# A forget bias carried as three rows of the score product, one constant causal mask, and keys loaded once a head pair, in forgetting attention followed by a channel mix

## The chip, the cores and the metric

The kernel runs on one core of a Trainium2 chip. Time is device microseconds for one execution. The core's engines are TensorE (PE in the profile; its weight loads, which overlap its products, are PEld), VectorE (DVE), ScalarE (ACT), GpSimd (POOL) and SyncE (SP), which issues all transfers of this kernel on one queue. SBUF is the on-chip memory of 128 partitions, PSUM the memory that TensorE writes its products to.

## The reference, cut to what matters

```python
batch, n_heads, seq, head_dim = 8, 8, 576, 64      # d_model 512, d_ff 1024
def attn(q, k, v, s):
    scores = q @ k.T / sqrt(64)
    cum = cumsum(max(s, 0), axis=-1)
    bias = -(cum[:, :, :, None] - cum[:, :, None, :])      # query position minus key position
    scores = where(causal, -1e9, scores + minimum(bias, 0))
    scores = scores - max(scores); a = exp(scores); a = a / (sum(a) + 1e-9)
    return a @ v
def channel_mix(x):                    # x: heads side by side, 512 wide
    xk, xr = mixes of x and x one token earlier
    v = max(xk @ w_k, 0) ** 2 @ w_v
    return sigmoid(xr @ w_r) * v
```

All is float32. As s is clipped at zero, cum never falls, so inside the causal triangle the bias is cum[key] - cum[query], and the part that depends on the query alone drops out of the softmax: only cum[key] has to be added to a row of scores.

## The kernel before, in words

**Work.** There are 32 head pairs (8 batches, 4 pairs each). Batch 0 is visited in two parts, tiles A = (0, 1, 2) for all four pairs (visits 0 to 3) and then Z = (3, 4) (visits 4 to 7); batches 1 to 7 are visited once a pair. A head has five query tiles, of 64, 128, 128, 128 and 128 queries, starting at 0, 64, 192, 320 and 448; tile t sees the keys up to its own end, 64, 192, 320, 448 and 576 of them. The last is cut in two score tiles of 288 keys, so there are six score tiles a head. From batch 3 on (`PAIRED`) the heads are of a kind in which tiles 2 and 4 keep the weights of their last 64 keys at the front of the tile (`front`), so that two transposes can be taken as one. The channel mix runs in 18 chunks of 256 tokens, a chunk as soon as its tokens are there; its products are lines 1165 (hidden), 1207 (gate) and 1232 (output).

**Precision.** A matrix product takes two roundings. Each operand is split into a high part, rounded to fp32r (the format for fast products), and a low part, the rest. `split_qk` (line 637) makes for each head KH (k rounded, ACT, line 645), KL (the rest, POOL, line 649) and G, whose upper 64 partitions hold the rounded q (ACT, line 656) and whose lower 64 the rest of q (POOL, line 660). A head has 64 rows, so q and k are loaded twice, once on each half of the partitions (`load_turned`, line 624). A score tile is the sum of two products, G with KH and G with KL, each over all 128 rows (line 730). Visits 0 to 3 go another way: plain float32 products (line 719) with queries padded by zeros, and keys that are loaded once a pair.

**Bias and mask.** `prefix_sums` computes cum for all 64 heads at the start and stores it to DRAM (`cum_d`). Each later head gets its row back by a transfer that repeats it on all partitions (`cb`, 288 KB, line 682); heads 0 and 1 compute theirs directly (`first_sums`), heads 2 to 7 of batch 0 get theirs in two early loads (line 1319). POOL makes from cb the head's masks: cb with a large negative number above the diagonal (line 701). VectorE then reduces each score tile (line 757): it adds a row of cb left of the diagonal block and a row of the mask inside it, writes the sum to W and keeps the minimum of the negated scores in `nm`. These are two instructions where a score tile holds both kinds of columns, and each is followed by a short one that reads the accumulator. The exponent (ACT, line 775), the reciprocal of the sums (POOL and DVE, lines 815 and 820), the normalisation (POOL, line 791), the transposes (PE, lines 837 and 937), their splits (ACT and DVE, lines 866 to 924) and the products with v (PE, lines 986 and 1000) follow.

**Order.** Nothing waits in program order as written: every operation is handed to `Plan` with an estimated cost, what it reads and writes, and a due time. `Plan.run` simulates the engines twenty times, and emits all instructions in the order of the best simulation, so the order on each engine is fixed before the kernel runs, and a changed cost or operation can change it everywhere. While TensorE has nothing to do before its first steady work, the plan fills in dummy products (line 398). Buffers are named by a tag and a count of copies: KH, KL and G have three each, `raw` four, `cb` and `mask` two, and a writer waits for the readers of the copy that it takes.

Of the kernel before, what the change touches and what calls it, by code (L numbers as in the profile page):

```python
# [312 lines left out]
def forgetting_attention_then_channel_mix(  # L313
# [139 lines left out]
    cum_d = fixed(dram.tile([B * H, S], F32, name="cum_d"))  # L453

    def prefix_sums():
        cum = sbuf([B * H, S], "mask", 2)
        spos = sbuf([B * H, S], "mask", 2)
# [20 lines left out]
        dma(lambda: nc.sync.dma_start(cum_d.ap, cum.get()), [cum], [cum_d], 410)  # L478

    def first_sums(nk):  # L480
# [3 lines left out]
        cbs = [sbuf([P, nk], "cb", 2) for _ in range(2)]  # L484
# [9 lines left out]
        for j in range(2):  # L494
            dve(
                lambda j=j: nc.vector.tensor_tensor_scan(
                    out=cbs[j].get(), data0=ones.get(), data1=raw.get()[:, j], initial=0.0,
                    op0=ALU.mult, op1=ALU.add,
                ),
                [ones, raw], [cbs[j]], 2 * nk,  # L500
            )
        return cbs
# [111 lines left out]
    def load_keys(b, hp, e):  # L614
        x = sbuf([P, e], "KH", 3)
# [8 lines left out]
    def load_turned(src, b, hp, a, e):  # L624

        xs = [sbuf([P, e - a], "raw", 4) for _ in range(2)]
        for j in range(2):
            for r in range(2):
                dma(
                    lambda j=j, r=r: nc.sync.dma_start(  # L630
                        xs[j].get()[64 * r : 64 * r + 64], src[b, 2 * hp + j, :, a:e]
# [5 lines left out]
    def split_qk(qs, ks):  # L637

        nq, nk = qs[0].n, ks[0].n
        G = [sbuf([P, nq], "G", 3, F32R) for _ in range(2)]  # L640
        KH, KL = ([sbuf([P, nk], x, 3, F32R) for _ in range(2)] for x in ("KH", "KL"))
        for j in range(2):
            k, kh, kl = ks[j], KH[j], KL[j]
            act(
                lambda k=k, kh=kh: nc.scalar.copy(kh.get(), k.get()),  # L645
                [(k, 0), (k, 1)], [(kh, 0), (kh, 1)], nk, 90,
            )
            pool(
                lambda k=k, kh=kh, kl=kl: nc.gpsimd.tensor_tensor(  # L649
                    out=kl.get(), in0=k.get(), in1=f32(kh.get()), op=ALU.subtract  # L650
                ),
                [(k, 0), (k, 1), (kh, 0), (kh, 1)], [(kl, 0), (kl, 1)], nk, 210, 2.21,
            )
            q, g = qs[j], G[j]
            act(
                lambda q=q, g=g: nc.scalar.copy(g.get(), q.get()),
                [(q, 0), (q, 1)], [(g, 0), (g, 1)], nq, 90,
            )
            pool(
                lambda q=q, g=g: nc.gpsimd.tensor_tensor(  # L660
                    out=g.get()[64:P], in0=q.get()[64:P], in1=f32(g.get()[64:P]), op=ALU.subtract
# [5 lines left out]
    def scores(b, h, tiles, G, KH, KL):  # L667
# [137 lines left out]
        if 0 in tiles:  # L805
            mask(64, 0, 1)
# [652 lines left out]
```

## Time and profile before

| | us |
|---|---|
| median of 3 runs (859.77 to 861.87) | 860.07 |
| the profiled execution | 860.73 |
| its span | 858.9 |
| PE busy | 844.9 |
| PEld busy | 748.7 |
| DVE busy | 676.3 |
| ACT busy | 679.2 |
| POOL busy | 494.5 |

The profile is of one execution. A group of instructions is given as line, engine, operation, out<-in, shape and count, then the busy time in us, the mean of one in ns, and the idle time of the engine ahead of them with what ended it. Shapes are partitions by elements; for a product they stand behind rows by columns of the array. A product is pipelined, so what it costs in a stream is the time from its start to the next start, and its own duration is longer. A wait is given as engine, line, what was waited for, then the sum in us, the count and the longest.

### The profile page before, as it was taken

Reading aid. Unit: us, or ns where it says so; the run is one execution under the profiler, and the core shown is the slowest. Engines: PE = TensorE matmul, PEld = TensorE weight load, DVE = VectorE, ACT = ScalarE, POOL = GpSimd, SP = SyncE. Lnnn points to the kernel's source line nnn. Section 1 sums busy time; section 2 is a strip of 40 time slices with the busy share of each in tenths; the row PEclk is TensorE's granted clock in tenths of the full one; section 3 lists DMA queues with packets and bytes.
Section 4 is the critical chain, followed back from the end, with each engine's and each line's share of the span. In section 5 each row is a group of like instructions: output and inputs, shape, how many; then the busy total and the mean of one; then the engine's idle time right before and its main releaser. Section 6 shows DMA issues by size and latency. Waiting matters only on the chain.

```text
span 858.9 us, 18405 instructions
## 1 busy us (share of the span) xinstructions
PE 844.9 (98%) x5541; PEld 748.7 (87%) x5541; DVE 676.3 (79%) x2425; ACT 679.2 (79%) x1850; POOL 494.5 (58%) x854
## 2 busy tenths in 40 slices
PE   9979999999999999999999999999999999999998
PEld 8659789889898898989898989898989989988996
DVE  6988889989877998789878887888888789455431
ACT  3998999999988898789979797978897878445331
POOL 5897899997766757466665566456665652000000
PEclk9999999999999999999999999999999999999999
DMA  8879655564443545335343435252534220210100
GB/s 249 257 236 265 192 164 166 166 184 141 148 136 111 144 124 156 96 112 158 110 128 118 136 104 158 77 149 84 168 98 135 86 92 15 64 33 18 50 26 24
DMA packets 63108, 109.04 MB, mean 127 GB/s; under 512 B 10144, under 2 KB 24480, under 8 KB 63008
## 3 DMA queue, kind: packets, MB, share of 16 engines
q1 hardware_dynamic: 63008, 107.87, 42.7%
q8 instruction: 43, 0.70, 0.3%
q14 instruction: 57, 0.47, 0.2%
HBM read 88.80 MB, written 19.04 MB: 126 GB/s over the span
## 4 chain that ended last, share of the span: by engine, by line
PE 91%; ACT 3%; DMA 2%; DVE 1%; issue 1%; POOL 1%; SPq 0%; ACTq 0%; POOLq 0%; DVEq 0%
PE m L1232 21%; PE m L1165 19%; PE s L730 10%; PE m L1207 10%; PE po L1000 9%; PE t L837 9%; PE t L1232 2%; PE po L398 2%; PE po L986 2%; PE s L1165 2%; PE t L1165 2%; PE t L1000 1%; PE t L937 1%; PE s L719 1%; DMA w_v<-in_moe_w_v 1%
## 5 line engine op out<-in xcount | busy, mean ns | idle before, releaser
L1165 PE MATMUL m<-xh,w_k 128*128 128x256 f32 x976 | 200.3, 286 | 0.0
L775 ACT ACTIVATE W<-W,nm 128x448 f32<-128x448 f32 (+4 forms) x320 | 179.9, 563 | 25.2 <-DVE nm L757 22.4
L1232 PE MATMUL m<-w_v,kh 128*128 128x512 f32 x528 | 188.1, 406 | 0.0
L791 POOL TENSOR_SCALAR W<-W,rinv 64x64 f32<-64x64 f32 (+4 forms) x320 | 164.3, 532 | 12.6 <-DVE rinv L820 10.6
L1165 PEld LDWEIGHTS m<-xh,w_k 128*128 128x128 f32 x976 | 158.8, 189 | 1.4 <-DVE kl L1194 0.2
L837 PE MATMUL t<-ident,W 128*128 128x128 f32 (+1 forms) x736 | 134.7, 276 | 6.4 <-ACT ph L866 2.7
L1165 PE MATMUL m<-xl,w_k 128*128 128x256 f32 x488 | 139.7, 286 | 0.0
L649 POOL TENSOR_TENSOR KL<-raw,KH 128x576 fp32r<-128x576 f32 x64 | 91.6, 1432 | 80.1 <-ACT KH L645 75.4
L870 DVE TENSOR_TENSOR pl<-t,ph 128x512 fp32r<-128x512 f32 x224 | 107.1, 485 | 12.7 <-ACT ph L866 10.7
L837 PEld LDWEIGHTS t<-ident,W 128*128 128x128 f32 (+1 forms) x736 | 89.3, 137 | 27.0 <-ACT ph L903 5.2
L1232 PEld LDWEIGHTS m<-w_v,kh 128*128 128x128 f32 x528 | 98.1, 189 | 15.3
L730 PE MATMUL s<-KH,G 128*64 128x64 f32 (+2 forms) x360 | 110.7, 312 | 0.3 <-DVE nm L757 0.3
L757 DVE CUSTOM_DVE_ANT_0 W<-s,cb 128x64 f32<-128x64 f32 (+1 forms) x244 | 92.1, 381 | 17.9 <-PE s L730 15.4
L1232 PE MATMUL m<-w_v,kl 128*128 128x512 f32 x264 | 105.7, 400 | 0.0
L730 PE MATMUL s<-KL,G 128*64 128x64 f32 (+3 forms) x360 | 105.5, 297 | 0.0
L866 ACT CAST ph<-t 128x512 fp32r<-128x512 f32 x224 | 93.1, 424 | 12.5 <-PE t L837 10.5
L660 POOL TENSOR_TENSOR G<-raw,G 64x576 fp32r<-64x576 f32 (+1 forms) x64 | 85.8, 1341 | 27.6 <-issue 10.2
L1111 DVE SCALAR_TENSOR_TENSOR xp<-x,mu,xp 128x256 f32<-128x256 f32 (+3 forms) x184 | 76.3, 415 | 25.0 <-ACT xp L1104 22.5
L1104 ACT ACTIVATE xp<-x,mu 128x256 f32<-128x256 f32 (+3 forms) x184 | 77.6, 422 | 21.4 <-DMA x<-x_d 12.1
L1165 PEld LDWEIGHTS m<-xl,w_k 128*128 128x128 f32 x488 | 92.2, 189 | 0.8 <-DVE xl L1137 0.3
L1207 PE MATMUL m<-w_r,xh 128*128 128x512 f32 x264 | 92.6, 402 | 0.0
L757 DVE CUSTOM_DVE_ANT_0 W<-s,mask,nm 128x128 f32<-128x128 f32 x256 | 86.7, 344 | 3.1 <-POOL mask L701 0.5
(154 smaller groups left out, 1934.0 us busy)
## 6 DMA issues: line engine op xcount, KB each, us to landing
raw<-in_k SPq DMA_DIRECT2D x128, 144.0 KB, 3.2
cb<-cum_d SPq DMA_DIRECT2D x64, 288.0 KB, 3.6
raw<-in_q SPq DMA_DIRECT2D x112, 144.0 KB, 3.7
out<-g SPq DMA_DIRECT2D x36, 256.0 KB, 2.6
vn<-in_v SPq DMA_DIRECT2D x28, 320.0 KB, 3.3
x_d<-xT SPq DMA_DIRECT2D x28, 288.5 KB, 2.5
x<-x_d SPq DMA_DIRECT2D x11, 514.0 KB, 4.6
w_k<-in_moe_w_k SPq DMA_DIRECT2D x8, 512.0 KB, 5.5
```

Source lines behind the costliest of these rows:

```text
L649: lambda k=k, kh=kh, kl=kl: nc.gpsimd.tensor_tensor(out=kl.get(), in0=k.get(), in1=f32(kh.get()), op=ALU.subtract),
L730: lambda x=x, K=K: nc.tensor.matmul(ps.get()[:m, :w], G.get()[:, q0 : q0 + m], K.get()[:, k0 : k0 + w], start=x == 0, stop=x == 1,),
L757: lambda a=a, e=e, row=row, i=i, to=to: nc.vector.tensor_tensor_reduce(out=to(), in0=ps.get()[:m, a - k0 : e - k0], in1=row()[:m, a:e], sc ...
L775: lambda: nc.scalar.activation(W.ap[:m, :n], W.ap[:m, :n], AF.Exp, bias=nm.get()[:m, 3 * t + mi : 3 * t + mi + 1], scale=-1.0, accum_out=s ...
L791: lambda: nc.gpsimd.tensor_scalar(out=to.ap[:m, c : c + n], in0=W.ap[:m, :n], scalar1=rinv.get()[:m, t : t + 1], scalar2=1.0, op0=ALU.mult ...
L837: lambda: nc.tensor.transpose(ps.get()[0:m, place : place + P], pt[t].ap[:, k0 + front(t, tiles) : k0 + front(t, tiles) + m], ident.ap,),
L866: act(lambda: nc.scalar.copy(strips(ph), src()), [ps], [(ph, k) for k in ks], n * m)
L870: lambda: nc.vector.tensor_tensor(out=strips(pl), in0=src(), in1=f32(strips(ph)), op=ALU.subtract),
L1000: lambda: nc.tensor.matmul(po.get()[: P if both else 64, at + q0 - base : at + q0 - base + m], V.get()[:, kb, 2 * j : 2 * j + (2 if both e ...
L1165: lambda u=u, f=f, c=c, n=n, w=w, x=x: nc.tensor.matmul(ps.get()[:, u * CT : (u + 1) * CT], weight["k", c, f // 4].get()[:, w, f % 4 * P : ...
L1207: lambda c=c, n=n, x=x, w=w: nc.tensor.matmul(ps.get(), x.get()[:, c, ts], weight["r", c, 0].get()[:, w], start=c == 0 and n == 0, stop=c ...
L1232: lambda f=f, n=n, x=x, w=w: nc.tensor.matmul(ps.get(), x.get()[:, f, ts], weight["v", f, 0].get()[:, w], start=f == 0 and n == 0, stop=f ...
```

## The change

- `prefix_sums` also splits each prefix sum into three fp32r parts (two copies on ACT, two subtractions on VectorE) and stores them to DRAM as `cum3_d`, three rows a head.
- For visits 4 and later, `split_qk` makes other operands. QQ holds the rounded q on both halves of the partitions; K holds the rounded k on one half and the rest of k on the other. QL has the rest of q on 64 partitions and ones on three more (set once a buffer); KB has k, rounded by VectorE, on 64 partitions and the head's three rows of prefix sums on three more, loaded by a 6.75 KB transfer. A score tile is QQ with K over 128 rows plus QL with KB over 67 rows, and then holds scores and bias.
- With the bias in the product, the mask is the same for all heads: `lower`, built once, zero below the diagonal and the large negative number above it in its last 128 columns. The reduction of a score tile adds a slice of it, in one instruction, or in two where the last 64 columns are written to the front of the tile. The bias rows and masks of a head go, except in visits 0 to 3, which keep them in other buffers.
- Keys are loaded once a pair, 64 partitions for each of the two heads, in one transfer of 288 KB (160 KB in visits 0 to 3, as before) in place of four of 144 KB.

```diff
@@ prefix_sums
+        parts = [sbuf([B * H, S], x, 1, F32R) for x in ("w_v_2_0", "w_v_3_0", "xh1")]
+        for i, x in enumerate(parts):
+            if i < 2:
+                act(lambda x=x: nc.scalar.copy(x.get(), cum.get()), [cum], [x], S, 90)
+                dve(
+                    lambda i=i, x=x: nc.vector.tensor_tensor(
+                        out=(parts[2] if i else cum).get(), in0=cum.get(), in1=f32(x.get()),
+                        op=ALU.subtract,
+                    ),
+                    [cum, x], [parts[2] if i else cum], S,
+                )
+            dma(
+                lambda i=i, x=x: nc.sync.dma_start(cum3_d.ap[:, 2 - i], f32(x.get())),
+                [x], [(cum3_d, i)], 410,
+            )
@@ split_qk(b, hp, qs, k)
+            own, other = slice(64 * j, 64 * j + 64), slice(64 - 64 * j, P - 64 * j)
+            QQ, K = (sbuf([P, n], x, 3, F32R) for n, x in ((nq, "G"), (nk, "KH")))
+            QL, KB = (sbuf([P, S], x, 3, F32R) for x in ("QL", "KL"))
+            if made[0] < 3:
+                made[0] += 1
+                ahead(lambda QL=QL: nc.vector.memset(f32(QL.get()[64:67]), 1.0), (QL, 1), S)
+            dma(
+                lambda j=j, KB=KB: nc.sync.dma_start(
+                    f32(KB.get()[64:67, 0:nk]), cum3_d.ap[b * H + 2 * hp + j, :, 0:nk]
+                ),
+                [(cum3_d, i) for i in range(3)], [(KB, 1)], 40,
+            )
             act(
-                lambda k=k, kh=kh: nc.scalar.copy(kh.get(), k.get()),
+                lambda own=own, K=K: nc.scalar.copy(K.get()[own], k.get()[own]),
...
             pool(
-                lambda k=k, kh=kh, kl=kl: nc.gpsimd.tensor_tensor(
-                    out=kl.get(), in0=k.get(), in1=f32(kh.get()), op=ALU.subtract
+                lambda own=own, other=other, K=K: nc.gpsimd.tensor_tensor(
+                    out=K.get()[other], in0=k.get()[own], in1=f32(K.get()[own]), op=ALU.subtract
...
+            dve(
+                lambda own=own, KB=KB: nc.vector.tensor_copy(KB.get()[0:64, 0:nk], k.get()[own]),
+                [(k, j)], [(KB, 0)], nk, 1.92, 150, (2 * j, 0),
+            )
...
             pool(
-                lambda q=q, g=g: nc.gpsimd.tensor_tensor(
-                    out=g.get()[64:P], in0=q.get()[64:P], in1=f32(g.get()[64:P]), op=ALU.subtract
+                lambda x=x, QQ=QQ, QL=QL: nc.gpsimd.tensor_tensor(
+                    out=QL.get()[0:64, 0:nq], in0=x.get()[0:64], in1=f32(QQ.get()[0:64]),
+                    op=ALU.subtract,
...
+            found.append(((QQ, K, P), (QL, KB, 67)))
@@ scores: products
-            for x, K in enumerate((KH, KL) if KL is not None else ()):
+            for x, (G, K, n) in enumerate(() if CB else passes):
...
-                        G.get()[:, q0 : q0 + m],
-                        K.get()[:, k0 : k0 + w],
+                        G.get()[:n, q0 : q0 + m],
+                        K.get()[:n, k0 : k0 + w],
...
+            off = S - P - QS[t] if QS[t] < k0 + w else -k0
+            last = k0 + w - (f if QS[t] < k0 + w else 0)
+            for a, e, to in ((k0, last, k0 + f), (last, k0 + w, 0)):
+                if a < e:
+                    reduce(
+                        a, e, to, lambda a=a, e=e: lower.ap[:m, off + a : off + e], [lower]
+                    )
@@ load
-            loaded[n] = load_turned(q, b, hp, q0, q1), load_turned(k, b, hp, 0, q1)
+            loaded[n] = load_twice(b, hp, q0, q1), load_keys(b, hp, q1, "raw", 4)
@@ after prepare(0)
+    ahead(lambda: nc.vector.memset(lower.ap, 0.0), lower, S)
+    pool(
+        lambda: nc.gpsimd.affine_select(
+            out=lower.ap[:, S - P : S], in_=lower.ap[:, S - P : S], pattern=[[-1, P]], base=0,
+            channel_multiplier=1, compare_op=ALU.is_ge, fill=MASK * ISCALE,
+        ),
+        [], [lower], P, 137,
+    )
```

`ahead` is a small helper that hands an operation to VectorE with the earliest due time; `load_twice` is `load_turned` for q alone; `reduce` is the reduction of line 757 as a function.

More of the change, by code (lines that the diff above doesn't have):

```diff
@@ L453, in forgetting_attention_then_channel_mix @@
     cum_d = fixed(dram.tile([B * H, S], F32, name="cum_d"))
+    cum3_d = fixed(dram.tile([B * H, 3, S], F32, name="cum3_d"))
+    lower = fixed(const.tile([P, S], F32, name="lower"))
     def prefix_sums():
-        cum = sbuf([B * H, S], "mask", 2)
-        spos = sbuf([B * H, S], "mask", 2)
+        cum = sbuf([B * H, S], "x")
+        spos = sbuf([B * H, S], "xl0")
         ones = sbuf([B * H, S], "raw", 4)
@@ L483, in first_sums @@
         ones = sbuf([P, nk], "raw", 4)
-        cbs = [sbuf([P, nk], "cb", 2) for _ in range(2)]
+        cbs = sbuf([P, 2, nk], "xh0")
         dma(
@@ L496, in first_sums @@
                 lambda j=j: nc.vector.tensor_tensor_scan(
[L497 removed]
+                    out=cbs.get()[:, j], data0=ones.get(), data1=raw.get()[:, j], initial=0.0,
                     op0=ALU.mult, op1=ALU.add,
                 ),
[L500 removed]
+                [ones, raw], [(cbs, j)], 2 * nk,
             )
[L502 removed]
+        return [(cbs, 0), (cbs, 1)]
     def load_mu():
@@ L635, in load_turned, with ahead @@
         return xs
[L637 to L641, printed above, removed]
-        for j in range(2):
-            k, kh, kl = ks[j], KH[j], KL[j]
-            act(
-                lambda k=k, kh=kh: nc.scalar.copy(kh.get(), k.get()),
-                [(k, 0), (k, 1)], [(kh, 0), (kh, 1)], nk, 90,
+    made = [0]
+    def ahead(emit, what, n):
+        due, plan.due = plan.due, -2.0e5
+        dve(emit, [], [what], n)
+        plan.due = due
@@ L766, in products @@
                     ),
-                    [ps, (bias, t > 0 if own else part)] + ([(nm, (t, i - 1))] if i else []),
+                    [ps] + reads + ([(nm, (t, i - 1))] if i else []),
                     [(W, i), (nm, (t, i))], e - a, extra=143 if i else 78,
@@ L770, in products @@
                 i += 1
+            if CB:
+                if k0 < QS[t]:
+                    reduce(k0, QS[t], k0, lambda: bias_row()[:m, k0 : QS[t]], [(CB, part)])
+                own = slice(QS[t], QS[t] + m)
+                reduce(own.start, own.stop, own.start, lambda: M.get()[:m, own], [(M, t > 0)])
+                return i
+            off = S - P - QS[t] if QS[t] < k0 + w else -k0
[5 more added lines that the diff above has]
+                    )
             return i
@@ L803, in rs @@
             return x.get()[:, tiles[0] : tiles[-1] + 1]
-        if 0 in tiles:
+        if CB:
             mask(64, 0, 1)
-        mask(P, QS[max(1, tiles[0])], len([t for t in tiles if t]))
+            mask(P, QS[1], len(tiles) - 1)
         for t in tiles:
```

78 lines of the change are left out of this document (32 added, 46 removed).

## The prediction

> **What bounds the kernel now.** I read the page first (engines, slices, chain), then busy time by stage, then the waits of TensorE, then single groups.
>
> ```profile
> span 858.9 us, 18405 instructions
> PE 844.9 (98%) x5541; PEld 748.7 (87%) x5541; DVE 676.3 (79%) x2425; ACT 679.2 (79%) x1850; POOL 494.5 (58%) x854
> ...
> DMA  8879655564443545335343435252534220210100
> ...
> PE 91%; ACT 3%; DMA 2%; DVE 1%; issue 1%; POOL 1%; SPq 0%; ACTq 0%; POOLq 0%; DVEq 0%
> ```
>
> TensorE (PE) is busy 98% of the span and holds 91% of the chain that ended last. A modelled busy time alone would not prove that it runs at its peak, so I compare two places in the chain of waits in order of time: one in the middle, where attention and the channel mix are interleaved, and one near the end, where only the channel mix is left.
>
> ```profile
> 524.17 2.82 PE m L1165 x24
> ...
> 772.37 2.82 PE m L1165 x24
> ```
>
> 24 products of the same kind take 2.82 us in both places, 0.118 us each: in the middle TensorE is already at the rate of its undisturbed tail. The stages follow (length, then busy time of PE, PEld, DVE, ACT, POOL, granted clock, DMA share, GB/s):
>
> ```profile
> 18.00:42.00 24.00, 23.04 (x147) 16.45 (x145) 22.09 (x96) 21.57 (x79) 21.02 (x54) 1.00 0.87 272
> 42.00:62.00 20.00, 13.81 (x68) 10.39 (x69) 18.55 (x55) 19.23 (x55) 18.29 (x24) 0.91 0.74 222
> 62.00:120.00 58.00, 57.44 (x352) 48.04 (x352) 47.51 (x164) 53.52 (x138) 50.06 (x75) 1.00 0.79 220
> 120.00:330.00 210.00, 209.59 (x1429) 188.43 (x1428) 187.20 (x739) 194.17 (x546) 161.74 (x273) 1.00 0.51 146
> 330.00:740.00 410.00, 409.71 (x2711) 368.91 (x2710) 340.46 (x1262) 340.94 (x941) 235.23 (x401) 1.00 0.38 113
> 740.00:858.90 118.90, 115.15 (x685) 101.45 (x683) 49.96 (x86) 43.03 (x83) 0.00 (x0) 1.00 0.10 33
> ```
>
> So there are two kinds of stage. Until about 62 us TensorE waits for others: in 42 to 62 us it is busy 13.8 of 20 us while ACT is busy 19.2, DVE 18.6 and POOL 18.3. From 120 to 740 us its visible gaps are 0.7 us of 620. After 740 us there is no attention left, POOL is empty, and nothing that the change touches runs. The sum of TensorE's work does not depend on how fast the heads are served: a head that is ready sooner only lets a channel-mix product run later. The end moves only by what TensorE gains or loses in waiting, and by a change of its own work.
>
> **The change part by part.** The sum goes against the profiled execution, 860.73 us (span 858.9 and 1.8 us around it); it lies 0.66 us above the median of 860.07.
>
> *TensorE's products.* Each score tile keeps two products of the same widths: first (high part of q) with (high and low part of k), over 128 rows; then (low part of q, and three rows of ones) with (k, and three rows of prefix sums), over 67 rows instead of 128. The width sets the time, so I take 0. The nearest rows for a product with fewer rows are the plain value products of 64 rows, against the same with 128:
>
> ```profile
> 43.30 0.33 PE L986 MATMUL po<-ph,V 128*128 128x64 f32 x2
> 43.44 0.38 PE L730 MATMUL s<-KH,G 128*128 128x288 f32 x1
> ...
> 81.01 0.43 PE L986 MATMUL po<-ph,V 64*128 64x64 f32 x2
> 81.38 0.33 PE L837 MATMUL t<-ident,W 128*128 128x128 f32 x1
> ...
> L730 PE MATMUL s<-KL,G 128*64 128x64 f32 (+3 forms) x360 | 105.5, 297 | 0.0
> ```
>
> From start to next start the 128-row pair takes 0.14 us and the 64-row pair 0.37: 0.23 us more for going into the smaller row count and out again. The bounds are thus 0 and 0.23 us for each of the 360 second products, 83 us, with no cover, since TensorE is full. I take 0: 64 rows are half of the array's 128, 67 are more than half. The Trainium skill (TensorEngine Tiling (Array Packing), Tiling Modes) says that a change of tiling mode drains TensorE, and lists modes of 128, 64 and 32 rows, with the smaller ones for contractions up to 64. The trace agrees for 64 rows; by that list 67 rows are no change of mode and the term is 0, and a mode taken from the bare row count would give the 83 us.
>
> *VectorE's reductions.* Bias and mask no longer differ along a row, so the piece below the diagonal block and the block itself become one instruction where the output is contiguous.
>
> ```profile
> L757 DVE CUSTOM_DVE_ANT_0 W<-s,mask,nm 128x128 f32<-128x128 f32 x256 | 86.7, 344 | 3.1 <-POOL mask L701 0.5
> L757 DVE DVE_READ_ACCUMULATOR2_ANT nm<- 128x1 f32 x576 | 47.1, 82 | 0.0
> L757 DVE CUSTOM_DVE_ANT_0 W<-s,cb 128x320 f32<-128x320 f32 x64 | 31.1, 486 | 4.5 <-PE s L730 4.1
> L757 DVE CUSTOM_DVE_ANT_0 W<-s,cb 128x192 f32<-128x192 f32 x58 | 20.4, 352 | 5.5 <-PE s L730 4.8
> ```
>
> 320 against 192 columns cost 134 ns more, 1.05 ns a column. Merging saves the separate block (344 + 82 ns) and adds 128 columns (134 ns): 0.29 us a merge. Merges: four a head in batches 1 and 2 (16 heads), two in the paired batches 3 to 7 (40 heads; there tiles 2 and 4 still write their last 64 columns elsewhere) and two in the eight heads of visits 4 to 7. That is 64 + 80 + 16 = 160 merges, 46.7 us less.
>
> *VectorE's new copy of k* into KB, 64 a run. The nearest row has the same shape, one source, both sides in SBUF:
>
> ```profile
> L465 DVE TENSOR_SCALAR mask<-mask 64x576 f32<-64x576 f32 x1 | 0.5, 504 | 5.9 <-DMA mask<-in_s 5.9
> ```
>
> 64 by 0.50 us is 32.3 us more (up to 48 if it goes at the 1.05 ns a column of a reduction plus its 150 ns). VectorE's net is 14 us less at 0.50, nothing at the upper bound; per head 0.67 us less in batches 1 and 2, 0.08 less in the others.
>
> *POOL.* The masks go; the subtraction for k keeps its 576 columns on half the partitions, and its rows show that the partitions do not matter:
>
> ```profile
> L649 POOL TENSOR_TENSOR KL<-raw,KH 128x576 fp32r<-128x576 f32 x64 | 91.6, 1432 | 80.1 <-ACT KH L645 75.4 <-DMA x<-x_d 3.0 <-DVE rinv L820 0.4
> L660 POOL TENSOR_TENSOR G<-raw,G 64x576 fp32r<-64x576 f32 x56 | 79.9, 1427 | 26.6 <-issue 10.2 <-ACT G L656 9.5 <-DMA vn<-in_v 2.5
> L701 POOL TENSOR_SCALAR_AFFINE_SELECT mask<-cb 128x512 f32<-128x512 f32 x56 | 35.4, 632 | 0.3
> L701 POOL TENSOR_SCALAR_AFFINE_SELECT mask<-cb 64x64 f32<-64x64 f32 x58 | 13.5, 233 | 14.7 <-DMA cb<-cum_d 9.2 <-DVE cb L496 3.7 <-DVE nm L757 0.3
> ```
>
> 56 by (632 + 233) ns is 48 us less; the eight masks of 256 columns for visits 4 to 7 lie between the two rows, 3 us together. ACT's copies keep their widths: 0.
>
> *Transfers.*
>
> ```profile
> raw<-in_k SPq DMA_DIRECT2D x128, 144.0 KB, 3.2
> cb<-cum_d SPq DMA_DIRECT2D x64, 288.0 KB, 3.6
> ```
>
> Keys: 128 issues of 144 KB become 32 of 288 KB, 9.4 MB less. Bias: 64 of 288 KB become 64 of 6.75 KB, 18 MB less. About a quarter of the page's 109 MB goes, and 96 of SP's issues. The new small transfer waits on SP for a KL buffer where the bias transfer waited for a cb buffer.
>
> *What of this reaches the end, after 62 us.* These are the waits of TensorE (first three) and of its weight loads (the rest) in 65 to 740 us that name what is relieved:
>
> ```profile
> PE t L937 <- POOL W L791: 0.4, 1, 0.4
> PE s L730 <- DVE nm L757: 0.3, 1, 0.3
> PEld t L837 <- DVE pl L870: 2.1, 9, 0.4
> PEld t L937 <- POOL W L791: 0.8, 2, 0.6
> PEld s L730 <- DVE nm L757: 0.8, 3, 0.5
> ```
>
> Together 4.4 us: that is the most that can go. The chunk work fills most of what a late head leaves, and the paired heads, 40 of 64, get only 0.08 us of VectorE each, so I take 1.5 us off (bounds 0 and 4.4). What is late next in these tiles is the exponent on ACT, which is untouched.
>
> *Before 62 us.* Added at the start are two copies on ACT, four memsets, two subtractions on VectorE, an affine select on POOL and three stores on SP:
>
> ```profile
> L645 ACT CAST KH<-raw 128x576 fp32r<-128x576 f32 x64 | 43.0, 672 | 1.4 <-DMA raw<-in_k 0.9 <-PE s L730 0.6
> ACT w_k L577 <- DVE xh L571: 3.9, 1, 3.9
> L1194 DVE TENSOR_TENSOR kl<-m,kh 128x512 fp32r<-128x512 f32 x61 | 41.8, 685 | 4.9 <-ACT kh L1192 4.3
> L463 POOL MEMSET raw<- 64x576 f32 x1 | 0.6, 575 | 0.0
> 8.37 0.48 SPq L478 DMA_DIRECT2D cum_d<-mask  x1
> 12.36 1.71 SPq L1319 DMA_DIRECT2D w_v<-cum_d  x2
> 61.46 0.28 PE L1165 MATMUL m<-xh,w_k 128*128 128x256 f32 x1
> ```
>
> The copies are casts of 576 columns, 1.3 us, inside ACT's idle 3.9 us. The memsets, at 0.58 us each as on POOL, are 2.3 us of the 5.9 us in which VectorE waits for its first transfer (the L465 row above); the select costs less than the 632 ns of the wide mask, in the 3.7 us in which POOL waits for the first cb (the 64x64 mask row). Not covered are the subtractions, which fall where VectorE has no gap: 685 ns for 512 columns give 0.75 us, 1.5 us for the two. The stores, of the size of the one at 8.37 us, take 0.48 us of issue each, 1.4 us, and may stand ahead of the early bias loads at 12.36 us, behind which further q, k and weight loads queue. Bounds of the delay: 0 and 2.9 us; I take 1.0, since weight conversion can move into the holes. It counts in full only if it reaches the first channel-mix product at 61.46 us: from there on TensorE is never short of work. Visits 4 to 7 lose 3 us of POOL and 3 MB of transfers, but ACT, busy 19.2 of 20 us, keeps all of its work: I take 0.5 us off, between 1 us more (a different order) and 6.2 us less (all of TensorE's loss in that stage).
>
> Sum: 860.7 + 1.0 - 0.5 - 1.5 = 859.7, less 0.66 to the median: 859 us.
>
> **The rivals.**
>
> *No cover was needed (faster).* ACT, DVE, POOL and the queue are all nearly full before 62 us and feed each other, so a quarter less traffic and 3 us less POOL may loosen ACT too. For it: the DMA share is 0.87 in 18 to 42 us. Against it: ACT's own busy time. The Trainium skill (SBUF — State Buffer, Who interferes with whom) says that a copy of VectorE in its two-port mode shuts POOL out of SBUF while it runs; by that the eight copies for visits 4 to 7, 4 us, would take back POOL's 3 us there, and no row of this trace shows it. With half of the 6.2 us, and 3 of the 4.4, and no delay at the start: 860.1 - 3.1 - 3 = 854 us.
>
> *The start gets slower.* The prefix parts stand in front of the first heads on VectorE and SP, and the chain until 62 us takes the delay on. It decides when, with no gain later, more than 2.6 us of the 2.9 and of the 1 us for reordered visits come through: with all of it 860.1 + 2.9 + 1 = 864 us.
>
> *67 rows drain the array.* Each second product is then 0.23 us longer with its neighbours, and from 0.01 us on it decides the sign: 860 + 83 = 943 us. For it are the 64-row rows; against it that 67 rows are more than half of the array.
>
> *It doesn't do what it says:* VectorE's copy eats the merges (48 against 46.7 us) and the end does not move: that is in the forecast's own range.
>
> **How the numbers follow.** About 0.3% (2.6 us) is what a measurement tells from no change. Forecast, 857.5 to 862.6 us: 0.41. Faster rival: 0.39. Slow start: 0.13. Drain: 0.07. The likeliest is no change with a lean to the fast side, 858.7 (own range 856 to 862); the range runs from a little beyond the faster rival, 851, to beyond the slow start, 866; the drain is left out.
>
> **What would show it.** Right: no cb and mask instructions after visit 3; DVE busy some 10 to 15 us lower, POOL about 50 lower, PE's count and busy share the same; about 82 MB moved; 24 L1165 products still in 2.82 us. The start is read from the first L1165 product, at about 61.5 us now: each us there is a us at the end. Wrong: a longer start-to-start around the 67-row products, a first L1165 product beyond 63 or before 58 us, or PE waiting for KB's small transfer, which the forecast leaves at nothing.

## The result, and the profile after

The changed kernel takes 873.67 us (median of four runs, 873.47 to 874.64) against 860.97 for the kernel before beside it (859.77 to 863.14): ratio 1.0147, 95% interval 1.0123 to 1.0171. It is 12.7 us slower, where 858.7 was forecast. The profile page's first lines and the chain that ended last, by engine and by line (a view names a buffer, so KB stands there as KL, QQ as G and K as KH):

```profile
span 872.0 us, 17614 instructions
PE 855.7 (98%) x5536; PEld 753.6 (86%) x5536; DVE 700.8 (80%) x2175; ACT 689.3 (79%) x1852; POOL 455.9 (52%) x735
...
PE 72%; DVE 5%; ACT 2%; issue 1%; POOL 0%; DVEq 0%; ACTq 0%; POOLq 0%
PE m L1270 18%; PE m L1203 16%; PE m L1245 9%; PE s L766 8%; PE po L1038 7%; PE t L875 6%; PE t L1270 2%; PE s L1203 2%; PE t L1203 2%; DVE KL L692 1%; DVE W L781 1%; PE t L1038 1%; DVE pl L908 1%; PE t L975 1%; PE po L1245 1%
```

Less work is done (POOL 38.6 us less; 81.55 MB moved, not 109), but VectorE rose from 676.3 to 700.8 us, and VectorE now has 5% of the chain, with the new copy of k (KL L692) by name. The stages, with the columns of before:

```profile
42.00:62.00 20.00, 16.97 (x71) 13.09 (x71) 19.41 (x49) 18.39 (x52) 17.61 (x23) 0.74 0.61 199
62.00:120.00 58.00, 57.26 (x357) 48.99 (x355) 51.63 (x129) 54.29 (x137) 46.58 (x62) 1.00 0.46 136
120.00:330.00 210.00, 206.81 (x1389) 183.03 (x1388) 190.01 (x610) 192.40 (x535) 142.43 (x223) 1.00 0.33 100
330.00:740.00 410.00, 407.64 (x2678) 364.49 (x2677) 344.53 (x1156) 342.03 (x934) 215.85 (x342) 1.00 0.26 80
```

The first channel-mix product of TensorE in order of time, and two places of the chain of waits:

```profile
59.17 0.78 PE L1203 MATMUL m<-xh,w_k 128*128 128x256 f32 x1
```

```profile
581.74 2.86 PE m L1203 x24
...
755.48 2.85 PE m L1203 x24
```

Nothing is lost at the start: the first channel-mix product (L1203, L1165 before) comes at 59.17 us, 2.3 us earlier. At 0.74 the granted clock of 42 to 62 us is below the 0.91 of before, and still the start is not later; from 62 to 740 us it is 1.00 in both. The rate holds too: 24 of these products take 2.86 us in the middle and 2.85 in the tail. The 2.82 of before is no faster rate, as the kernel before has such groups of 2.85 and 2.87 too (at 576.58 and 625.56 us). From 120 to 740 us TensorE does 73 products fewer than the kernel before (4067 against 4140): it has lost time. Its visible gaps grew from 0.7 to 5.6 us, and the rest sits in waits that no gap shows, because a product's record (0.28 us for 256 columns) is longer than its 0.12 us of the stream. I add those up as *lost time*: from 120 to 745 us, each product's start to the next one's start, less what a product of its kind takes in an undisturbed stream (0.118 us for 256 columns, 0.134 for 288). Before 19.9 us, after 34.1: 14.2 more, about the 12.7 of the result. Only differences of this sum are used. The waits of TensorE and then of its weight loads, 65 to 740 us (sum in us, count, longest):

```profile
PE po L1038 <- DVE pl L908: 1.6, 4, 0.9
PE t L875 <- DVE xT L1076: 1.4, 2, 1.0
PE t L1038 <- DVE pl L908: 1.2, 1, 1.2
```

```profile
PEld po L1038 <- DVE pl L908: 4.6, 10, 1.3
PEld t L875 <- DVE pl L908: 2.9, 13, 0.3
PEld po L1038 <- ACT ph L904: 2.9, 13, 0.4
PEld t L875 <- DVE xT L1076: 2.7, 4, 1.4
```

These waits are for VectorE and ScalarE, in the steps after the softmax, few of which the change touches: ph and pl are the high and the low part of the transposed weights, xT is a head's output on its way to the channel mix. So something stands ahead of these steps in the queues of those engines. The 64 new copies by their line (shortest, median and longest in ns), and around the longest gap the chain of waits and the order of time on VectorE, GpSimd and TensorE:

```profile
L692 DVE CAST KL<-raw x64: 415/472/2917, 34.9 to 701.3; 64x576 fp32r<-64x576 f32 x64
```

```profile
208.53 1.99 DVE KL L692
```

```profile
208.45 2.07 DVE L692 CAST KL<-raw 64x576 fp32r<-64x576 f32 x1
210.64 0.28 DVE L908 TENSOR_TENSOR pl<-t,ph 128x128 fp32r<-128x128 f32 x1
...
206.88 1.67 POOL L829 TENSOR_SCALAR W<-W,rinv 128x448 f32<-128x448 f32 x3
208.50 1.71 POOL L621 TENSOR_TENSOR V<-vn,V 128x320 fp32r<-128x320 f32 x2
210.16 1.62 POOL L701 TENSOR_TENSOR QL<-raw,G 64x576 fp32r<-64x576 f32 x1
...
210.97 0.33 PE L1038 MATMUL t<-ph,V 128*128 128x128 f32 x1 [1.25 <-DVE pl L908]
```

Half of the copies take under half a microsecond, this one 2.07. It comes while a GpSimd instruction (L829) runs until 208.54, then waits out two subtractions that follow without a gap and end at 210.21, and ends 0.31 us after them; pl behind it starts at 210.64, and TensorE has stood 1.25 us for it. The 2917 ns copy lies beside two GpSimd instructions in the same way, and ends 0.3 us after the second. So it goes with nearly all: 24 copies take over 0.7 us, and 23 of them end 0.31 to 0.33 us after the end of a GpSimd instruction. Of the 12 places where the sum above loses over 0.25 us at once (7.2 us; before 2 places, 1.0 us), nine come within 4 us after a copy that took over 0.8 us.

### The profile page after: what moved, and what is told of

Read it like the earlier page. It is cut to its first block, busy times and chain, and to the rows that moved or that the text cites. A ratio compares the mean times of both kernels' runs of the same rounds, so it can differ in the third digit from the quotient of the medians.

```text
span 872.0 us, 17614 instructions
## 1 busy us (share of the span) xinstructions
PE 855.7 (98%) x5536; PEld 753.6 (86%) x5536; DVE 700.8 (80%) x2175; ACT 689.3 (79%) x1852; POOL 455.9 (52%) x735
## 2 busy tenths in 40 slices
DMA packets 48877, 81.55 MB, mean 94 GB/s; under 512 B 7824, under 2 KB 22160, under 8 KB 48784
## 4 chain that ended last, share of the span: by engine, by line
PE 72%; DVE 5%; ACT 2%; issue 1%; POOL 0%; DVEq 0%; ACTq 0%; POOLq 0%
PE m L1270 18%; PE m L1203 16%; PE m L1245 9%; PE s L766 8%; PE po L1038 7%; PE t L875 6%; PE t L1270 2%; PE s L1203 2%; PE t L1203 2%; DVE KL L692 1%; DVE W L781 1%; PE t L1038 1%; DVE pl L908 1%; PE t L975 1%; PE po L1245 1%
## 5 line engine op out<-in xcount | busy, mean ns | idle before, releaser
L1203 PE MATMUL m<-xh,w_k 128*128 128x256 f32 x976 | 205.8, 288 | 0.1
L813 ACT ACTIVATE W<-W,nm 64x64 f32<-64x64 f32 (+4 forms) x320 | 179.4, 562 | 26.1 <-DVE nm L781 21.8
L829 POOL TENSOR_SCALAR W<-W,rinv 128x192 f32<-128x192 f32 (+4 forms) x320 | 166.6, 539 | 25.4 <-DVE rinv L858 20.8
L1203 PEld LDWEIGHTS m<-xh,w_k 128*128 128x128 f32 x976 | 160.6, 189 | 2.9 <-DVE kl L1232 0.7
L781 DVE CUSTOM_DVE_ANT_0 W<-s,lower 128x288 f32<-128x288 f32 (+1 forms) x296 | 121.7, 420 | 23.3 <-PE s L766 21.4
L1203 PE MATMUL m<-xl,w_k 128*128 128x256 f32 x488 | 139.2, 286 | 0.0
L875 PE MATMUL t<-ident,W 128*128 128x128 f32 (+1 forms) x736 | 131.8, 276 | 4.3 <-DVE xT L1076 1.4
L686 POOL TENSOR_TENSOR KH<-raw,KH 64x576 fp32r<-64x576 f32 x64 | 93.4, 1460 | 80.6 <-ACT KH L682 35.9
L766 PE MATMUL s<-KH,G 128*64 128x64 f32 (+1 forms) x360 | 109.4, 311 | 1.7 <-DVE nm L781 1.7
L766 PE MATMUL s<-KL,QL 67*64 67x64 f32 (+1 forms) x360 | 107.2, 302 | 0.3 <-DVE KL L692 0.3
L1203 PEld LDWEIGHTS m<-xl,w_k 128*128 128x128 f32 x488 | 92.5, 189 | 1.3 <-DVE xl L1175 0.3
L701 POOL TENSOR_TENSOR QL<-raw,G 64x576 fp32r<-64x576 f32 (+1 forms) x64 | 87.2, 1363 | 11.5 <-ACT G L697 9.0
L621 POOL TENSOR_TENSOR V<-vn,V 128x320 fp32r<-128x320 f32 x56 | 48.8, 889 | 72.9 <-ACT V L617 68.2
```

Source lines behind the costliest of these rows:

```text
L686: lambda own=own, other=other, K=K: nc.gpsimd.tensor_tensor(out=K.get()[other], in0=k.get()[own], in1=f32(K.get()[own]), op=ALU.subtract),
L701: lambda x=x, QQ=QQ, QL=QL: nc.gpsimd.tensor_tensor(out=QL.get()[0:64, 0:nq], in0=x.get()[0:64], in1=f32(QQ.get()[0:64]), op=ALU.subtract,),
L766: lambda x=x, G=G, K=K, n=n: nc.tensor.matmul(ps.get()[:m, :w], G.get()[:n, q0 : q0 + m], K.get()[:n, k0 : k0 + w], start=x == 0, stop=x == 1,
L781: lambda i=i: nc.vector.tensor_tensor_reduce(out=W.ap[:m, to : to + e - a], in0=ps.get()[:m, a - k0 : e - k0], in1=row(), scale=-SCALE, sc ...
L813: lambda: nc.scalar.activation(W.ap[:m, :n], W.ap[:m, :n], AF.Exp, bias=nm.get()[:m, 3 * t + mi : 3 * t + mi + 1], scale=-1.0, accum_out=s ...
L829: lambda: nc.gpsimd.tensor_scalar(out=to.ap[:m, c : c + n], in0=W.ap[:m, :n], scalar1=rinv.get()[:m, t : t + 1], scalar2=1.0, op0=ALU.mult ...
```

## The experiments

The theory that I began with: VectorE's copy waits for GpSimd, unevenly, and TensorE pays. The rivals: the copy costs by being VectorE time at all; the cost lies elsewhere in the change. All medians below stand beside runs of the kernel before at 861.0 to 861.7 us, so a difference of two of them is good to about 1 us. Where an edit changes what the planner is told, it orders all engines anew; e12 and e8 (against after), e13 (e9), e14 (after), e15 (e1) and e3 (e2) keep every instruction at its place, the others don't. In the table, lost time is the sum defined above. The edits are cut to the lines that matter.

| run | us | ratio to before (95%) | lost time, us | DVE, us | ACT, us |
|---|---|---|---|---|---|
| before | 860.97 | | 19.9 | 676.3 | 679.2 |
| after | 873.67 | 1.0147 (1.0123 to 1.0171) | 34.1 | 700.8 | 689.3 |
| e1_k_by_dma | 866.72 | 1.0061 (1.0046 to 1.0076) | 26.7 | 659.3 | 687.6 |
| e2_scratch_cast | 881.96 | 1.0235 (1.0219 to 1.0250) | 37.1 | 707.6 | 688.3 |
| e3_scratch_memset | 871.20 | 1.0121 (1.0104 to 1.0138) | 29.1 | 689.1 | 687.2 |
| e4_cast_on_act | 880.69 | 1.0226 (1.0208 to 1.0244) | 37.5 | 660.3 | 722.8 |
| e5_two_reductions | 866.86 | 1.0066 (1.0051 to 1.0081) | 25.6 | 680.4 | 687.9 |
| e6_before_other_order | 861.77 | 1.0004 (0.9993 to 1.0014) | 20.9 | 676.7 | 679.5 |
| e7_e1_other_order | 872.34 | 1.0131 (1.0114 to 1.0148) | 29.8 | 662.0 | 688.3 |
| e8_cast_by_max | 881.82 | 1.0239 (1.0224 to 1.0255) | 41.8 | 717.4 | 690.3 |
| e9_e1_three_first | 863.97 | 1.0032 (1.0021 to 1.0044) | 22.8 | 658.9 | 685.6 |
| e10_before_three_first | 861.69 | 0.9999 (0.9989 to 1.0008) | 21.0 | 676.5 | 679.1 |
| e11_after_three_first | 873.35 | 1.0137 (1.0122 to 1.0152) | 33.4 | 702.8 | 688.1 |
| e12_cast_by_reduce | 868.95 | 1.0088 (1.0073 to 1.0103) | 29.1 | 699.7 | 689.1 |
| e13_whole_cast_e9 | 860.61 | 0.9994 (0.9986 to 1.0003) | 20.2 | 659.7 | 680.5 |
| e14_whole_cast_after | 873.29 | 1.0141 (1.0128 to 1.0155) | 33.3 | 700.1 | 684.2 |
| e15_whole_cast_e1 | 864.51 | 1.0042 (1.0027 to 1.0057) | 24.2 | 659.7 | 683.3 |
| e16_three_edits | 865.66 | 1.0040 (1.0028 to 1.0052) | 26.3 | 697.7 | 682.7 |
| e17_true_cost | 863.79 | 1.0020 (1.0011 to 1.0030) | 22.3 | 697.7 | 683.9 |

**The copy, taken away or put elsewhere.** In e1 KB's rows of k come by a transfer from K; e2 adds to e1 a useless cast of VectorE, e3 a useless memset at the same place and planned cost; e4 gives the copy of the changed kernel to ScalarE.

```diff
# e1, in split_qk
-            dve(lambda ...: nc.vector.tensor_copy(KB.get()[0:64, 0:nk], k.get()[own]), ...
+            dma(lambda ...: nc.sync.dma_start(f32(KB.get()[0:64, 0:nk]), f32(K.get()[own])),
+                [(K, j)], [(KB, 0)], 410 * nk / S)
# e2, on top of e1: tensor_copy of k to QL[96:128]; e3, on top of e1:
+            dve(lambda QL=QL: nc.vector.memset(f32(QL.get()[96:P, 0:nk]), 0.0),
+                [(k, j)], [(QL, 3)], nk, 1.92, 150, (2 * j, 3))
# e4, on the changed kernel
-            dve(lambda ...: nc.vector.tensor_copy(KB.get()[0:64, 0:nk], k.get()[own]), ...
+            act(lambda ...: nc.scalar.copy(KB.get()[0:64, 0:nk], k.get()[own]), ...
```

> The changed kernel, but the 64 rows of k in KB come from K (already rounded by ACT) by a transfer on SP inside SBUF, 144 KB a head, and VectorE's cast of k is gone. Theory A (the cast waits for POOL's instruction in flight, holds up VectorE's queue, and TensorE then waits for VectorE): DVE busy falls by 45 to 50 us to about 653, the waits of TensorE and its weight loads on DVE pl fall to what they were before the change, and the time is 854 to 861 us. Rival B (the new order made by the planner, with single reductions, is worse by itself): 868 to 875 us. Rival C (SP's queue, which now waits for a KL buffer, is what delays): 873 us or more, since SP gets one more transfer a head with one more wait.

> e1, and in the place of the removed cast VectorE casts 576 columns of k, on 32 partitions, into rows of QL that nobody reads. Planned at the same cost as the cast of the changed kernel. Theory A: the casts last 0.45 us when POOL is idle and up to 2.9 us when it is not, mean about 0.74 as in the changed kernel, and the time is back at 868 to 875 us. Rival A2 (VectorE's 30 to 47 us more of busy time, not the waiting for POOL, is what counts): the same time as e3_scratch_memset within 2 us. Rival B: the same as e1 within 2 us.

> e2 with a memset of the same 576 columns and 32 partitions in place of the cast: an instruction of VectorE with the same planned cost, the same place and about 0.6 us of its time, but without a source in SBUF. Theory A: every memset lasts 0.55 to 0.65 us, whatever POOL does, and the time is 856 to 863 us, clearly below e2. Rival A2: as e2, 868 us or more, as its busy time is about the same. Rival B: as e1.

> The changed kernel with the cast of k for KB on ACT in place of VectorE: 64 more casts of 0.67 us, 43 us more of ACT. Theory A: no cast waits for POOL, the waits on DVE fall, but ACT, which is full until about 200 us, gets 43 us more: 858 to 869 us. Rival B: 870 us or more. Rival C: unchanged against the changed kernel, 872 to 875 us or more.

Without the copy 7.0 of the 12.7 us are gone, a little over half: 866.7 us lies between the theories. The order is another one too, so this alone does not show what the copy costs. The memset costs 4.5 us over e1, the cast 15.2. Both overshoot the ranges of their theory A, e2 by 7 us and e3 by 8, and how much of that is their order is open. Between the two only the 64 instructions differ, and the cast is 10.8 us dearer. It also takes 18.5 us more of VectorE, and in e2's profile the granted clock is halved for 3.4 us at 184 us, at most 1.7 us by my estimate. The rows of the cast in e2 and of the memset in e3 (shortest, median, longest in ns) show how the two differ:

```profile
L699 DVE CAST QL<-raw x64: 452/552/2012, 51.4 to 706.8; 32x576 fp32r<-32x576 f32 x64
```

```profile
L698 DVE MEMSET QL<- x64: 538/538/538, 50.7 to 695.2; 32x576 f32 x64
```

No memset is ever longer than 538 ns, whatever GpSimd does; the cast is. On ScalarE the copy costs more than on VectorE: 880.69 us, 12 above theory A's range. Much of it is lost in one place, here in e4 and in the kernel before (columns as in the stages):

```profile
160.00:180.00 20.00, 14.17 (x88) 11.47 (x87) 13.15 (x40) 18.88 (x46) 15.64 (x23) 0.95 0.43 124
```

```profile
160.00:180.00 20.00, 20.00 (x129) 17.22 (x127) 17.63 (x77) 19.73 (x60) 18.40 (x31) 1.00 0.51 151
```

ScalarE is full there even before (19.73 of 20 us), and in e4 TensorE stands for 5.8 of the 20 us: ScalarE is no free engine here.

**The copy in two other forms, every instruction at its place.** e8 writes it as a two-input instruction, e12 as a reduction over an axis of length 1, which has one input. Both are planned at the cost of the copy, so only the form of 64 instructions differs from the changed kernel.

```diff
-                lambda own=own, KB=KB: nc.vector.tensor_copy(KB.get()[0:64, 0:nk], k.get()[own]),
# e8
+                lambda own=own, KB=KB: nc.vector.tensor_tensor(
+                    out=KB.get()[0:64, 0:nk], in0=k.get()[own], in1=k.get()[own], op=ALU.max
# e12
+                lambda own=own, KB=KB: nc.vector.tensor_reduce(
+                    out=KB.get()[0:64, 0:nk], in_=k.get()[own].rearrange("p (x o) -> p x o", o=1),
+                    axis=mybir.AxisListType.X, op=ALU.max,
```

> The changed kernel (873.7 us) with the copy of k into KB written as a two-input tensor_tensor (max of k with itself, the same values), planned at the same cost, so that every instruction keeps its place and only the form of 64 instructions on VectorE changes. Theory A (the copy waits for GpSimd because of its form, a lock of the port that both use, and its waiting is what costs): the two-input form takes 0.65 to 0.75 us each whatever GpSimd does, none over 1 us, and the time is 866 to 870 us. Theory B (it is busy time on VectorE or the copy's place that costs): 873 to 876 us, and long instructions stay.

> The changed kernel with the copy of k into KB written as a tensor_reduce (max) over an axis of length 1: one SBUF input and one element a cycle; planned at the same cost, so that every instruction keeps its place. The two-input form of e8 took 0.71 us alone and still waited for GpSimd (up to 2.8 us). Theory A (the copy waits for GpSimd where it takes the port that GpSimd uses; a form that does not take it, as the memset of e3, never waits): 64 instructions of 0.62 to 0.72 us, none over 0.8, 40 to 46 us in all against the cast's 47.2, and with the long ones gone 867 to 871 us. Theory B (what counts is VectorE's time, however it is spread): 872 to 874 us.

The 64 instructions by their line, in e8 and in e12, and their group (busy us, mean ns) in the changed kernel and in e12:

```profile
L692 DVE TENSOR_TENSOR KL<-raw x64: 709/796/2815, 34.6 to 708.9; 64x576 fp32r<-64x576 f32 x64
```

```profile
L692 DVE TENSOR_REDUCE KL<-raw x64: 704/746/751, 35.0 to 696.6; 64x576 fp32r<-64x576 f32 x64
```

```profile
L692 DVE CAST KL<-raw 64x576 fp32r<-64x576 f32 x64 | 47.2, 737 | 1.0
```

```profile
L692 DVE TENSOR_REDUCE KL<-raw 64x576 fp32r<-64x576 f32 x64 | 47.5, 743 | 1.0
```

My expectation for e8 was wrong: a form with both inputs in SBUF waits for GpSimd as well, up to 2815 ns. The Trainium skill (SBUF — State Buffer, Who interferes with whom) says so: VectorE and GpSimd share a port pair, and whichever comes first holds it for its whole instruction. That goes for VectorE's copies in the two-port mode, and for its two-input instructions against a GpSimd instruction that reads SBUF; reductions, and other instructions with at most one SBUF input outside those modes, stay out of it. The rows of e2, e3, e8 and e12 agree. e12 is the clean test. Its instructions take 47.5 us in all, the copy's 47.2; none is longer than 751 ns, the copy's go to 2917. Same order, same VectorE time, 4.7 us less: this part of the loss is the waiting of the two engines for each other, and not VectorE's time. GpSimd is relieved as well (448.4 us busy for 455.9), but the waits of TensorE and its weight loads that name GpSimd in the changed kernel are 0.7 us in all, so I take the uneven copy for the cause; the runs don't part the two sides.

**What was left without the copy: 5 us.** Candidates were the merged reductions, which are longer (e5 cuts them at the diagonal block again), and the order alone (e6 and e7: one constant of the planner changed in the kernel before and in e1).

```diff
# e5, on e1: for a, e in ((k0, min(k0 + w, QS[t])), (max(k0, QS[t]), k0 + w)), as in the kernel before
# e6 on the kernel before, e7 on e1
-    DEPTH, WAIT = 6, 150.0
+    DEPTH, WAIT = 6, 140.0
```

> The kernel of e1_k_by_dma (KB's key rows by transfer, no cast on VectorE, 866.7 us), with the reductions cut at the own block again as in the kernel before: 576 instead of 480 tensor_tensor_reduce (counting the early heads), the constant mask kept. It looks for the 5 us by which e1 is still over the kernel before. Theory A (a merged reduction is longer, 0.62 us for 448 columns, so a bank of scores is given back later and what waits for it comes late): 860 to 863 us. Theory B (the merging is a gain or nothing; the 5 us lie in the order of the instructions or in the queue of transfers): 867 to 872 us, as VectorE gets 96 to 160 instructions of about 0.29 us back, up to 47 us of busy time, of which a tenth showed in the time when 45 us of scratch memsets were added (e3: 4.5 us over e1).

> The kernel before with one constant of the planner's choice of the next product changed (WAIT 150 to 140): the same instructions in a slightly other order. It measures what order alone is worth. Theory A (the order of the kernel before is a lucky one, and any change of the task list loses it): 863 to 868 us. Theory B (order alone is worth little): 859.5 to 863 us, within 0.2% of the kernel before.

> The kernel of e1_k_by_dma with the same constant changed (WAIT 150 to 140). Theory A (e1's 5 us over the kernel before are a matter of order): it moves by over 2 us, to 861 to 864.5 or above 869. Theory B (they are a cost that any order pays): 865 to 868.5 us.

The reductions give no sign of being it: 160 instructions more (640 for 480; the 576 of the expectation is a miscount) and 21.1 us more of VectorE, in a new order, change nothing (866.86 against 866.72). The order moves the kernel before by nothing and e1 by 5.6 us, to 872.34, nearly the changed kernel's time. So e1 is brittle, and what is read from one order of it is uncertain by as much. I followed where TensorE waits in e1: from 120 us on two of the five waits that the view names, 0.5 of 1.1 us, are for VectorE's small subtractions for pl (L964). In order of time in e1, and the group with the idle time ahead of it in the kernel before and in e1:

```profile
444.50 0.64 ACT L943 CAST ph<-t 64x128 fp32r<-64x128 f32 x3
445.17 0.59 ACT L906 CAST ph<-t 128x512 fp32r<-128x512 f32 x1
445.18 0.41 DVE L964 TENSOR_TENSOR pl<-t,ph 64x128 fp32r<-64x128 f32 x2 [0.30 <-ACT ph L943]
```

```profile
L924 DVE TENSOR_TENSOR pl<-t,ph 64x64 fp32r<-64x64 f32 (+2 forms) x152 | 34.7, 245 | 9.2 <-ACT ph L903 7.6
```

```profile
L964 DVE TENSOR_TENSOR pl<-t,ph 64x64 fp32r<-64x64 f32 (+2 forms) x152 | 34.8, 246 | 19.3 <-ACT ph L943 17.9
```

By what the planner was told, the first of them needs only the first of ScalarE's three casts. It starts behind the third, here and in 39 of the 40 paired heads, in 28 of them within 0.04 us of its end. This is so in the kernel before too (39 of 40, and 21), but there VectorE stood 7.6 us for ScalarE ahead of that line, in e1 17.9: as I read it, an emptier VectorE is planned right behind the first cast and stands idle until the third. e9, e10 and e11 tell the planner.

```diff
-                corner(0, k0, n, 2, at)
-                corner(0, 0, 0, 1, at)
-                corner(1, k0 + 1, n, 2, at)
+                parts = (0, k0, n, 2, at), (0, 0, 0, 1, at), (1, k0 + 1, n, 2, at)
+                for lows in [corner(*x) for x in parts]:       # corner issues the cast, lows the subtractions,
+                    lows([(ph, ("h", x)) for x in (0, *range(k0, k0 + 2 * n))])   # which read all three
```

> The kernel of e1_k_by_dma (866.7 us), with one thing told to the planner: in the paired heads VectorE's first subtraction for pl (L964) needs all three of ScalarE's small casts to ph (L943), not only the one whose strip it reads. In the trace of e1 it starts only after the third cast (445.18 us, casts at 444.50, 444.67 and 444.88), 0.4 us later than planned, and VectorE stands idle 17.9 us in all ahead of L964 (7.6 us in the kernel before). Theory A (e1's 5 us over the kernel before are this wait, met more often because VectorE has less to do): VectorE's idle time ahead of that line falls to under 8 us and the time is 860 to 863.5 us. Theory B (it is only where a loss shows that has another cause): 865 to 868 us.

> The kernel before (861 us) with the same thing told to its planner, as the control of e9. Both theories: the wait is 7.6 us of idle time on VectorE there and mostly harmless, so the time is within 2 us of the kernel before, 859 to 863 us. Under 858 us would mean that any kernel gains by it, and that e9's gain says nothing of the change.

> The changed kernel (873.7 us, the cast on VectorE kept) with the same thing told to its planner. Theory A (in the changed kernel the cast's waits for GpSimd cost most, and VectorE's idle time ahead of L962 is only 5.5 us): 871 to 874 us. Theory B (the same wait costs the changed kernel as much as e1): 867 to 870 us.

e9 gains 2.75 us, about half of what was open, and lands between its theories; the control does not move. The idle time for ScalarE ahead of the line fell only to 12.6 us, not under 8 as expected. That the wait was the cause is not shown: the edit moves other instructions too, and e7 has as much of this idle time as e1 (17.3 us) and is 5.6 us slower. In the changed kernel, where VectorE is fuller, the edit is worth 0.3 us.

**The last part: a cast of ScalarE on the upper half of the partitions.** The copies of k to KH that follow each other directly with the copy of q, in e1 (an even head, then an odd one) and in e13 (an odd head):

```profile
458.78 0.66 ACT L682 CAST KH<-raw 64x576 fp32r<-64x576 f32 x1
459.35 0.67 ACT L699 CAST G<-raw 128x576 fp32r<-128x576 f32 x1
...
416.57 0.67 ACT L682 CAST KH<-raw 64x576 fp32r<-64x576 f32 x1
417.26 0.67 ACT L699 CAST G<-raw 128x576 fp32r<-128x576 f32 x1
```

```profile
439.26 0.66 ACT L682 CAST KH<-raw 128x576 fp32r<-128x576 f32 x1
439.83 0.67 ACT L699 CAST G<-raw 128x576 fp32r<-128x576 f32 x1
```

Start to start the even head's cast takes 0.57 us, the odd head's, on partitions 64 to 127, 0.69. The odd casts also start 0.11 to 0.13 us late behind their predecessors: in e1 all 32 start after the end of the instruction ahead, most of the even ones about 0.1 us before it. Twice some 0.12 us for 32 odd casts make about 8 us of ScalarE. In e13, e14 and e15 the cast covers all 128 partitions again, as in the kernel before, in an unchanged order of instructions; GpSimd then overwrites the other half, as it does anyway.

```diff
-                lambda own=own, K=K: nc.scalar.copy(K.get()[own], k.get()[own]),
-                [(k, j)], [(K, j)], nk, 90,
+                lambda K=K: nc.scalar.copy(K.get(), k.get()),
+                [(k, 0), (k, 1)], [(K, 0), (K, 1)], nk, 90,
```

> The kernel of e9_e1_three_first (864.0 us), with ScalarE's cast of k into KH over all 128 partitions again, as in the kernel before, and not over the own 64 (GpSimd writes the other 64 afterwards, as now). Same order of every instruction. In the trace of e1 the cast of the odd head (partitions 64 to 127) starts 0.11 to 0.13 us later after the instruction ahead of it than the even head's, and what follows it starts 0.13 us later; in the kernel before neither head's cast has such a pause. 32 such casts make some 8 us of ScalarE's time. Theory A (these pauses are what is left of the loss): 861 to 862.5 us, level with the kernel before. Theory B (ScalarE has room for them): 863.3 to 864.7 us.

> The changed kernel (873.7 us) with the same edit alone. Theory A: 1 to 3 us less, 870.5 to 872.7 us. Theory B: 873 to 874.5 us.

> The kernel of e1_k_by_dma (866.7 us) with the same edit alone, in e1's order. Theory A: 1 to 3 us less, 863.7 to 865.7 us. Theory B: 866 to 867.4 us.

e13 is 860.61 us, level with the kernel before (0.9994, interval 0.9986 to 1.0003), and its lost time is 20.2 us, as before. From e9 the edit is worth 3.4 us, from e1 2.2, from the changed kernel 0.4: the causes don't add. I take it that one engine that is late hides another.

**VectorE's own time.** e16 keeps the copy on VectorE, in the form of e12, with the two other edits; e17 plans it at its measured duration (rate 0.96 for 1.92).

> The changed kernel with three edits together: the copy of k into KB as the tensor_reduce of e12 (868.95 us alone), the cast of k into KH over all 128 partitions (e13), and the planner told that the first pl subtraction needs all three small casts (e9). KB's rows still come from VectorE, 47.5 us of it. Theory A (VectorE's time is worth little once nothing waits unevenly): 860.5 to 863 us. Theory B (47.5 us more on VectorE cost by themselves, 2.2 us or more as between e1 and e12, and the two other edits are worth less beside it, as e11 and e14 were 0.3 and 0.4 us): 866 to 869 us.

> e16_three_edits with the copy planned at 0.75 us, what it takes in e12's trace (0.743 us), and not at 0.45 us. Theory A (an order planned with the true duration keeps VectorE's work out of the way): 1 to 4 us under e16. Theory B (the planned cost hardly matters): within 1 us of e16.

Between the two theories: 865.66 us with a wrong planned duration, 863.79 with the right one, 5.1 and 3.2 us above e13, which has no copy on VectorE. Part of the 3.2 goes with the granted clock: e17's three runs at 0.997 and 0.998 take 862.0 to 862.2 us, its nine below that 863.1 to 864.7, and e13's runs stand at 0.996 and 0.997. So 38 us more of VectorE, with nothing that blocks, may cost 1.5 to 5 us, but these are single orders, and 21.1 us more cost nothing in e5. No version beat both kernels; e13, with 17 us less VectorE and 45 us less GpSimd than the kernel before, is level with it, as TensorE was already full there (98% of the span).

## Why the prediction was wrong

- **Start.** The 1.0 us of delay did not come; the first L1203 product was 2.3 us earlier. The rival "the start gets slower" falls, and the faster rival was right about this stage alone.
- **TensorE's products.** Term 0, right; what the Trainium skill lists as tiling modes (TensorEngine Tiling (Array Packing), Tiling Modes) held. Start to start is 0.14 and 0.13 us around the 67-row product; the drain rival falls:

```profile
212.07 0.29 PE L766 MATMUL s<-KH,G 128*128 128x288 f32 x1
212.21 0.29 PE L766 MATMUL s<-KL,QL 67*128 67x288 f32 x1
212.34 0.28 PE L1203 MATMUL m<-xl,w_k 128*128 128x256 f32 x1
```

- **VectorE's reductions.** As durations the 46.7 us came out to the digit (273.9 to 227.2 us on their line). As engine time they are 21.1 us (e5's 680.4 less e1's 659.3), because the next instruction starts before the last one's duration ends. The sum of durations was the wrong quantity.
- **VectorE's copy.** Taken at 0.50 us; half of the copies take 0.42 to 0.47, but its mean is 737 ns and its longest 2917. With the reductions this makes VectorE's net 24.5 us more, not 14 less. The row that it was priced by (L465) ran at the start and showed no wait.
- **The port was read in one direction.** I quoted the Trainium skill (SBUF — State Buffer, Who interferes with whom) for a copy that shuts GpSimd out, which was to take back 3 us before 62 us, and left out that the copy is what waits when GpSimd is first, in front of everything else in VectorE's queue. Here that was the larger side in time: the copies take 47.2 us, 20.6 more than 64 times the shortest, and GpSimd is busy 7.5 us more than in e12.
- **ScalarE: 0, "keep their widths".** Wrong by about 8 us of ScalarE, 0.4 to 3.4 us of the kernel's time: the widths stayed, the partitions moved.
- **After 62 us, the step that failed.** I took 1.5 us off with bounds 0 and 4.4, as if the change could only take waits away. TensorE lost 14.2 us more there. "The chunk work fills most of what a late head leaves" does not hold for an instruction of 1 to 3 us ahead of pl and xT, which a stream of products is already waiting for: with the copy in a form that does not wait, and all else the same, 4.7 us are back. For the rest the runs name ScalarE's pauses and, less surely, the order. No rival had this mechanism, and 866 as the upper end held only delays at the start.
- **GpSimd and transfers.** 38.6 us less for 51 forecast (46.1 in e12, without the waiting), 81.55 MB for 82. Both were worth nothing, as e13 shows (450.0 us of GpSimd for 494.5, 91.0 MB for 109.0, and the same time); no wait of TensorE for KB's small transfer shows.

Taken away one after another, the 12.7 us go as 7.0 for the copy (after against e1), 2.75 for the wait that the planner did not know and 3.4 for ScalarE's pauses; in another order the shares differ. Shown with every instruction at its place are 4.7 us for the copy's waiting (e12) and 0.4 to 3.4 for the pauses (e13 to e15). The other steps each changed the order, and order alone moved e1 by 5.6 us, so the share of the planner's wait, and of VectorE's time by itself, stays open. Open is too why e2 and e3 are slower than expected.

## What to carry to other kernels

Where one engine is full and the others have slack, ask of each new instruction not only what it takes alone but whom it can stand behind, and for how long: 47 us with a longest instruction of 0.75 us cost 4.7 us less than the same 47 us with some of 2 to 3. Before an operation goes to VectorE beside a busy GpSimd, look for a form that did not wait here: a reduction (704 to 751 ns), or an input in PSUM (the kernel before has 61 subtractions kl<-m,kh of 669 to 693 ns). And give a loss bound as well as a gain bound wherever an order is made by a planner: what the planner does not know (an instruction that blocks, a pause, a wait) shows up elsewhere, under other lines' names. Two kernels that a planner ordered apart differ by their order as well; keep the order fixed where a cause is to be shown.

## What the runs showed of the hardware

- VectorE's copy from SBUF to SBUF (fp32 to fp32r, 64x576): 415 ns at the shortest, up to 2917 beside GpSimd; 23 of the 24 over 0.7 us end 0.31 to 0.33 us after a GpSimd instruction. The two-input form: 709 to 2815. The reduction form: 704 to 751. A memset of 32x576: 538, always.
- GpSimd pays as well: its subtraction for k has a mean of 1460 ns in the changed kernel (L686), 1422 without the copy and 1547 in e8.
- ScalarE's casts on partitions 64 to 127, between instructions that begin at partition 0, started 0.11 to 0.13 us late in e1, and so did their successors (0.69 us start to start for 0.57).
- A product of 288 columns over 67 rows takes 0.13 us of the stream, as one over 128 does.
